# A state-space block feeding a gated feed-forward block: weights taken in every second column, output weights in rows of two, and an earlier order of loads

## The chip, the cores and the metric

The kernel runs on one core of one Trainium2 chip. The metric is device time in microseconds (us) of one execution; times given for a kernel are medians over its runs. A core has TensorE (PE in the profile; PEld is its loading of weights), VectorE (DVE), ScalarE (ACT), GpSimd (POOL) and SyncE (SP). SP, ACT and POOL also issue DMA transfers: SP and ACT on hardware queues, POOL on a software queue, which can convert the type on the way.

## The reference

First a chunked state-space scan over x (4 batches, 8 heads, 768 positions, 32 values per head), with a decay `a` per position and B and C of 16 values per position:

```python
L = np.exp(cum[:, :, :, None] - cum[:, :, None, :]) * causal
M = np.einsum('bhin,bhjn->bhij', Cc, Bc) * L
y_intra = np.einsum('bhij,bhjd->bhid', M, xc)
y_inter = np.einsum('bhin,bhnd->bhid', Cc, state) * decay_to_i[:, :, :, None]
y[:, :, sl] = y_intra + y_inter
```

The heads of a position are then laid side by side (3072 tokens of 256 values), and a gated feed-forward layer follows, with d_ff = 1536:

```python
gate = np.maximum(x @ w_gate, 0.0)
val = x @ w_val
out = gate * val @ w_out
```

Inputs and output are float32; the kernel computes in bf16 with float32 sums.

## The kernel before, in words

**Tiles.** The 3072 tokens are 12 *pairs* of 256 tokens (two chunks of 128), and 6 *blocks* of 512 tokens (two pairs). The scan is done by pairs, the feed-forward layer by blocks. d_ff is cut into 12 tiles `f` of 128 columns. `wg` and `wv` are the gate and value weights in SBUF, shaped [128, 2, 1536]: 128 partitions, the two halves `k` of d_model, and d_ff. `wo` is the output weights, [128, 12, 256].

**The scan of a pair p** is a row of small helpers: `scale_bc` scales B and C by the decay factors (DVE or POOL), `turn` transposes them on PE, `tevac` copies them out, `back` transposes B back, `G` multiplies C with B (8 matmuls), `gevac` masks the result (ACT copies quarters 0 and half of 1, which POOL masks at L174; DVE masks the others), `Dm` multiplies with x, `inter` adds the state, `yevac` writes the pair's columns of `yT`. `astep`, `states`, `sevac` and `spread` carry the state.

**The feed-forward layer of a block.** `gv(b, f)` makes gate and val of tile f for 512 tokens (L595, L598, two matmuls of 512 columns each, one for each half k); `gvh_mm(b, f, u)` does it for a half block of 256 tokens (L614, four matmuls), which the kernel uses where only one pair of a block is ready. ACT takes the relu, DVE multiplies into `h`. `fout(b, ts)` multiplies `h` with `wo` (L643), 12 tiles f for each 128 tokens.

**The order** is written out by hand: every engine's instructions run in the order in which the program emits them (`in_order`, L15). The stretch that the change touches is the opening (L677 to L809) and block 0 of the loop at L811. In the opening, pairs 0 and 1 are scanned, and the half blocks `gvh_mm(0, f, 0)` for f = 0 to 3 stand between their steps, so that PE has work: f = 0 ahead of `G(1)` (L765), f = 1 after it (L773). Block 0 then goes on with f = 0 to 3 of its other half, f = 4 to 11 with `gv`, and `fout`, between whose steps the scans of pairs 2 and 3 stand.

**The loads.** POOL issues the weights on the software queue, float32 to bf16: f 0-1 and 2-3 at L229, f 4-5 at L743, f 6-8 and 9-11 at L771, each as one transfer for gate and one for val, which covers both halves k; after that POOL scales B and C of pair 2 (L787) and issues the output weights in three transfers of four f (L788). Behind them it issues x of pair 2 (`cast_x`, L808), converted by the transfer itself. SP loads the other x, B and C as float32; `held` (L707) lets them wait for a small DVE memset. x is then cast by an engine (`x_cast`, `to_x`).

**Waits.** The framework sets the semaphores: for each instruction it compares what it reads and writes with what was emitted earlier, and lets it wait where they overlap. The transfers of the software queue use eight semaphores in turn.

Of the kernel before, what the change touches and what calls it, by code (L numbers as in the profile page):

```python
# [29 lines left out]
def kernel(  # L30
# [43 lines left out]
    def place(p):  # L74
        b, c0 = p // PPB, 2 * (p % PPB)
        return b, c0, slice(c0 * 128, (c0 + 2) * 128)
# [58 lines left out]
    def new_xb(p):  # L135
        xb = att.tile([128, 2 * NH * D], BF16, tag="xb", name="xb", bufs=6)
        st.setdefault(p, {})["x"] = [xb[:, i * NH * D:(i + 1) * NH * D] for i in range(2)]

    def cast_x(p):

        b, c0, sl = place(p)
        new_xb(p)
        for i in range(2):
            sl = slice((c0 + i) * 128, (c0 + i + 1) * 128)
            nc.gpsimd.dma_start(
                out=st[p]["x"][i].rearrange("s (h d) -> s h d", d=D),
                in_=x[b, :, sl, :].rearrange("h s d -> s h d"))

    ident = const.tile([128, 128], BF16)
    make_identity(nc, ident)  # L150

# [4 lines left out]
    def weights(f0, f1, which=(0, 1)):  # L156
        fs = slice(f0 * 128, f1 * 128)
        for k in which:
            w, src = ((wg, moe_w_gate), (wv, moe_w_val))[k]
            nc.gpsimd.dma_start(  # L160
                out=w[:, :, fs], in_=src[:, fs].rearrange("(k p) f -> p k f", k=2))

    def weights_out(f0, f1):
        nc.gpsimd.dma_start(
            out=wo[:, f0:f1, :],
            in_=moe_w_out[f0 * 128:f1 * 128, :].rearrange("(o i) m -> i o m", i=128))

    masks = const.tile([128, 2, 128], BF16)

# [286 lines left out]
    def sevac(p, i):  # L456
        c = 2 * p + i + 1
        if c == NC:
            return
        if c < 2 * NTILE:  # L460
            S[c] = n = att.tile([128, 64], BF16, tag="Sd", name="Sd")
            nc.scalar.copy(out=n, in_=A_ps[0][:, 0, 0:64])
        else:
            S[c] = spread_one(c, 0)
# [124 lines left out]

    def gv(b, f):  # L590
        tk = slice(b * 512, (b + 1) * 512)
        fs = slice(f * 128, (f + 1) * 128)
        g, v = bank("gate"), bank("val")
        for k in range(2):
            nc.tensor.matmul(out=g, lhsT=wg[:, k, fs], rhs=yT[:, k, tk],  # L595
                             start=(k == 0), stop=(k == 1))
        for k in range(2):
            nc.tensor.matmul(out=v, lhsT=wv[:, k, fs], rhs=yT[:, k, tk],  # L598
                             start=(k == 0), stop=(k == 1))
        r = ffn.tile([128, 512], BF16, tag="r", name="r", bufs=4)  # L600
        nc.scalar.activation(r, g, AF.Relu)  # L601
        nc.vector.tensor_tensor(out=fst[b][:, f], in0=r, in1=v, op=ALU.mult)  # L602

    def gvh_mm(b, f, u):
        if f == 0 and u == 0:
            fst[b] = ffn.tile([128, NF, 512], BF16, tag="h", name="h")
        tk = slice(b * 512 + u * 256, b * 512 + (u + 1) * 256)
        fs = slice(f * 128, (f + 1) * 128)
        gv_ = (mm.tile([128, 2, 256], FP32, tag="y", name="gv") if b + f == 0 else
               bank("gv", (128, 2, 256)))  # L610
        jk = [(j, k) for j in range(2) for k in range(2)]
        early = b + f + u == 0
        for j, k in sorted(jk, key=lambda v: v[1]) if early else jk:
            nc.tensor.matmul(out=gv_[:, j], lhsT=(wg, wv)[j][:, k, fs], rhs=yT[:, k, tk],  # L614
                             start=(k == 0 and not (early and j)), stop=(k == 1),
                             skip_group_check=True)
        fst[b, f, u] = gv_
# [81 lines left out]
    def x_cast(p, i, eng):  # L699
        copy(eng, st[p]["x"][i], st[p]["xr"][:, i].rearrange("s h d -> s (h d)"))  # L700
# [6 lines left out]
    def held(p, bc=True, with_x=True):  # L707

        if bc:
            new_bc(p)  # L710
            nc.vector.memset(st[p]["bcr"][0:1, 0, 1, 0, 0:1], 0.0)
            load_bc(p, 1, nc.sync)
            load_bc(p, 0, nc.sync)
        if with_x:
            new_x(p)
            if not bc:
                nc.vector.memset(st[p]["xr"][0:1, 0, 0, 0:1], 0.0)
            for i in range(2):
                load_x(p, i, nc.sync)
# [8 lines left out]

    gevac(0, between=lambda: backevac(0, nc.scalar), after={2: load_x1})
    held(2, with_x=False)  # L730
    d12 = mm.tile([128, 2, 2, 8], FP32, tag="tp", name="d12")
    dec_wide(d12, pick[:, 1:3, 0:8])
    nc.scalar.copy(out=wfac[:, 1:3, 1].rearrange("p w r h -> p r w h"), in_=d12)
# [7 lines left out]
    scale_bc(1, nc.vector, B_, ts=(0,))  # L741
    scale_bc(1, nc.gpsimd, B_, ts=(1,))
    weights(4, 6)  # L743
    new_xb(1)

    x_cast(1, 0, nc.gpsimd)
    Dm(0, "shared")
    inter(0, 1)
    astep(0, 1)
# [2 lines left out]
    yevac(0, nc.scalar, nc.vector)  # L752
    bevac(1, nc.scalar)
    cevac(1, nc.vector)
    sevac(0, 1)

    def turn(p):
        transp(p, 1)
        transp(p, 0)
# [8 lines left out]
    back(1)  # L768
    gevac(1, early=True, between=lambda: backevac(1, nc.scalar))
    x_cast(1, 1, nc.scalar)  # L770
    weights(6, 9)  # L771
    weights(9, NF)
    gvh_mm(0, 1, 0)  # L773
    gvh_relu(0, 1, 0)
    gvh_mm(0, 2, 0)
# [9 lines left out]
    nc.vector.reciprocal(wfac[:, 2:4, 0], wfac[:, 2:4, 1])  # L785
    new_bs(2)
    scale_bc(2, nc.gpsimd)  # L787
    weights_out(0, 4)  # L788
    weights_out(4, 8)
    weights_out(8, NF)  # L790
    Dm(1, "shared")
    inter(1, 0)
    inter(1, 1)
# [11 lines left out]
            out=fac[:, :, 2 * w:2 * w + 2, 1, :].rearrange("p b i h -> p i b h"),  # L805
            in_=dall[:, :, w])
    new_bs(3)
    cast_x(2)  # L808
    scale_bc(3, nc.gpsimd)  # L809

    for b in range(NBLK):  # L811
        P, Q, W = 2 * b + 2, 2 * b + 3, 2 * b + 1
        more = P < NPAIR
        for n in (P + 2, P + 3):
            if b and n < NPAIR:
                load(n, nc.sync)

        nh = (4, 6, 5)[min(b, 2)]
        for f in range(nh):
            if b == 0:  # L820
                continue
            turning = f == (3 if b == 1 else 2)
            gvh_mm(b, f, 0)
            gvh_relu(b, f, 0)
            gvh_mul(b, f, 0)
            if turning:
                inter(W, 0)
                inter(W, 1)
                Dm(W)
                if more:  # L830
                    states(P)
                yevac(W, nc.scalar)
                if more:
                    spread(P)
        for f in range(nh):
            gvh(b, f, 1)
        for f in range(nh, NF):
            gv(b, f)
            if b == 0:
                if f == 5:  # L840
                    over_sum(de)
                if f == 6:
                    turn(P)
                    tevac(P, nc.scalar, nc.vector)
                if f == 8:
                    sevac(1, 1)
                if f == 9:
                    held(Q, bc=False)
                    back(P)
                    backevac(P, nc.scalar)  # L850
            elif more:
                if f == max(5, nh):
                    turn(P)
                    tevac(P, nc.scalar, nc.vector)
                    scale(Q, nc.gpsimd)
                if f == 8:
                    turn(Q)
                    tevac(Q, nc.scalar, nc.vector)
                    if Q + 1 < NPAIR:
                        scale(Q + 1, nc.gpsimd)  # L860
        if more and b:
            inter(P, 0)
            inter(P, 1)
        if b == 0:

            for third in range(3):
                fs = range(4 * third, 4 * third + 4)
                fout(b, 0, fs)
                fout(b, 1, fs)
                if third == 0:  # L870
                    held(Q + 1)
                if third == 1:
                    G(P)
                    gevac(P)
                    to_x(Q, nc.gpsimd)
            turn(Q)
            tevac(Q, nc.scalar, nc.vector)
            foevac(b, 1)
            state(P, 0)
            state(P, 1)  # L880
            held(Q + 2)
            def recip(n):
                nc.vector.reciprocal(fac[:, n, :, 0], fac[:, n, :, 1])

            recip(1)
            fout(b, 2)
            back(Q)
            backevac(Q, nc.vector)
            recip(2)
            recip(3)  # L890
            inter(P, 0)
            inter(P, 1)
        else:
            fout(b, 0)
            foevac(b, 0)
            if more:
                G(P)
                gevac(P)
            fout(b, 1)
            foevac(b, 1)  # L900
            fout(b, 2)
            foevac(b, 2)
        if more:
            Dm(P)
            states(Q)
            yevac(P, nc.scalar)
            G(Q)
            spread(Q)
            gevac(Q)
            if b == 0:  # L910
                scale(Q + 1, nc.gpsimd)
            fout(b, 3)
            foevac(b, 3)
        else:
            fout_last(b)
# [32 lines left out]
```

## Time and profile before

| | |
|---|---|
| median of 3 runs | 127.87 us (126.57 to 130.34) |
| the profiled execution | 127.37 us, of which the span from its first to its last instruction is 125.6 us |
| PE, DVE, ACT, POOL busy | 119.2, 95.1, 79.5, 44.0 us |
| granted TensorE clock | 1.00 in every stretch |
| software queue (q0) | 6384 packets, 2.49 MB |
| hardware queue of SP (q1) | 64512 packets, 8.57 MB |

How to read the profile: times are from the span's start. The span is cut into 40 slices of 3.14 us, and a digit is the busy share of a slice in tenths. A line of the timeline has start, duration, engine, line of the kernel, operation, what it writes and reads, how many were merged (x8) and, in brackets, how long the engine stood idle before it and what released it. Matmuls overlap, so that the time from one start to the next says more than the duration of one. A line of the chain that ended last has start, duration and what the end of the program hung on in that time. "To landing" is the time from the issue of a transfer until its data are reported as there.

### The profile page before, as it was taken

How to read it: one execution, taken by the hardware profiler on the slowest of the kernel's cores; microseconds unless marked ns; L12 is line 12 of the kernel's file. 1: busy time of each engine (PE TensorE's matmuls, PEld its weight loads, DVE VectorE, ACT ScalarE, POOL GpSimd, SP SyncE). 2: the span in 40 equal slices, each digit the busy share in tenths (PEclk: the TensorE clock that was granted, in tenths of full speed). 3: DMA queues.
4: the chain of work that ended last, by engine and by line, in shares of the span. 5: the costliest groups of instructions: out<-in, count | busy, mean ns of one | idle time of the engine just before them, and what ended most of it. 6: DMA issues, size and time to landing. Idle time of an engine off the chain costs nothing.

```text
span 125.6 us, 3450 instructions
## 1 busy us (share of the span) xinstructions
PE 119.2 (95%) x1282; PEld 83.3 (66%) x1288; DVE 95.1 (76%) x236; ACT 79.5 (63%) x181; POOL 44.0 (35%) x83
## 2 busy tenths in 40 slices
PE   7899999978999999999999999999999999999990
PEld 2566844556886567885477885577874577864790
DVE  5888789939999955898865998865898856697510
ACT  4167876523888734888745787725887645886410
POOL 5869969404624153713102805021700033000000
PEclk9999999999999999999999999999999999999999
DMA  3999999998969998386952289912200002200022
GB/s 68 191 185 161 134 196 198 175 116 79 178 69 189 97 123 127 106 123 93 94 83 89 85 87 125 111 23 84 89 0 0 0 0 85 87 0 0 5 84 84
DMA packets 74464, 12.00 MB, mean 96 GB/s; under 512 B 67040, under 2 KB 74448, under 8 KB 74448
## 3 DMA queue, kind: packets, MB, share of 16 engines
q1 hardware_dynamic: 64512, 8.57, 43.2%
q0 software_dynamic: 6384, 2.49, 17.1%
q10 hardware_dynamic: 3552, 0.72, 2.8%
q8 instruction: 10, 0.16, 0.6%
q14 instruction: 6, 0.05, 0.1%
HBM read 11.12 MB, written 3.15 MB: 114 GB/s over the span
## 4 chain that ended last, share of the span: by engine, by line
PE 75%; DMA 14%; DVE 5%; POOL 2%; issue 1%; SPq 1%; ACT 0%; DVEq 0%; POOLq 0%
PE o L643 22%; PE gv L614 19%; PE val L598 12%; PE gate L595 11%; DMA wo<-in_moe_w_out_dram 6%; DMA bcr<-in_B_dram 5%; PE g L406 3%; DMA bcr<-in_C_dram 3%; PE y L569 3%; PE tp L342 2%; DVE gs L429 2%; PE y L558 2%; PE o L655 1%; DVE bs L310 1%; POOL bs L310 1%
## 5 line engine op out<-in xcount | busy, mean ns | idle before, releaser
L643 PE MATMUL o<-wo,h 128*128 128x256 bf16 x276 | 33.2, 273 | 1.1 <-DMA wo<-in_moe_w_out_dram 1.1
L602 DVE TENSOR_TENSOR h<-r,val 128x512 bf16<-128x512 bf16 x42 | 28.6, 685 | 5.2 <-ACT r L601 2.9
L643 PEld LDWEIGHTS <-h 128*128 128x128 bf16 x276 | 25.9, 98 | 6.6 <-issue 3.3
L601 ACT ACTIVATE r<-gate 128x512 bf16<-128x512 f32 x42 | 25.1, 597 | 7.8 <-PE gate L595 6.9
L624 DVE TENSOR_TENSOR h<-r,gv 128x256 bf16<-128x256 bf16 x60 | 24.5, 419 | 3.0 <-ACT r L621 2.3
L174 POOL TENSOR_SCALAR_AFFINE_SELECT gs<-gs 128x512 bf16<-128x512 bf16 (+1 forms) x24 | 12.1, 527 | 40.5 <-ACT gs L418 40.5
L598 PE MATMUL val<-yT,wv 128*128 128x512 bf16 x84 | 25.0, 379 | 0.5
L621 ACT ACTIVATE r<-gv 128x256 bf16<-128x256 f32 x60 | 22.9, 386 | 2.5 <-PE gv L614 0.3
L595 PE MATMUL gate<-yT,wg 128*128 128x512 bf16 x78 | 23.7, 379 | 0.0
L614 PE MATMUL gv<-yT,wg 128*128 128x256 bf16 x120 | 23.1, 273 | 0.0
L614 PE MATMUL gv<-yT,wv 128*128 128x256 bf16 x120 | 23.0, 273 | 0.0
L429 DVE TENSOR_TENSOR gs<-g,masks 128x512 bf16<-128x512 f32 x24 | 15.4, 683 | 6.8 <-PE g L406 6.8
L310 POOL TENSOR_TENSOR bs<-bcr,fac 128x256 bf16<-128x256 f32 x16 | 9.6, 620 | 16.1 <-DMA bcr<-in_B_dram 16.1
L598 PEld LDWEIGHTS <-wv 128*128 128x128 bf16 x84 | 8.1, 98 | 10.3 <-DMA wv<-in_moe_w_val_dram 0.6
L418 ACT CAST gs<-g 128x512 bf16<-128x512 f32 x12 | 7.1, 589 | 10.6 <-PE g L406 10.6
L614 PEld LDWEIGHTS <-wv 128*128 128x128 bf16 x120 | 11.7, 98 | 1.4
L614 PEld LDWEIGHTS <-wg 128*128 128x128 bf16 x120 | 11.2, 98 | 1.7 <-issue 0.2
L284 ACT CAST yT<-y 128x512 bf16<-128x512 f32 (+1 forms) x14 | 7.1, 527 | 7.7 <-PE y L569 4.5
L595 PEld LDWEIGHTS <-wg 128*128 128x128 bf16 x84 | 7.8, 98 | 6.3
L672 ACT COPY ob<-o 128x512 f32<-128x512 f32 x10 | 5.9, 586 | 4.2 <-PE o L643 4.2
L284 POOL CAST xb<-xr 128x512 bf16<-128x512 f32 (+1 forms) x11 | 6.3, 573 | 3.2 <-DMA xr<-in_x_dram 2.5
L368 DVE TENSOR_SCALAR CT<-tp,tmask 128x256 bf16<-128x256 bf16 x23 | 7.0, 343 | 0.1
(102 smaller groups left out, 111.5 us busy)
## 6 DMA issues: line engine op xcount, KB each, us to landing
xr<-in_x_dram SPq DMA_DIRECT2D x21, 128.0 KB, 3.3
out_dram<-ob SPq DMA_DIRECT2D x10, 256.0 KB, 2.2
bcr<-in_C_dram SPq DMA_DIRECT2D x16, 64.0 KB, 3.1
bcr<-in_B_dram SPq DMA_DIRECT2D x16, 64.0 KB, 3.0
wo<-in_moe_w_out_dram POOLq DMA_DIRECT2D x3, 256.0 KB, 7.0
bcr<-in_C_dram SPq DMA_DIRECT2D x3, 128.0 KB, 6.1
bcr<-in_B_dram SPq DMA_DIRECT2D x3, 128.0 KB, 6.3
wg<-in_moe_w_gate_dram POOLq DMA_DIRECT2D x3, 128.0 KB, 4.4
```

Of the source, the lines that this page charges most:

```text
L174: nc.gpsimd.affine_select(out=dst, in_=dst, pattern=pattern, compare_op=ALU.is_ge, fill=0.0, base=0, channel_multiplier=-1)
L284: (eng.copy if eng is nc.scalar else eng.tensor_copy)(out=out, in_=in_)
L310: eng.tensor_tensor(out=dst[:, :, t], in0=src[:, :, t], in1=f[:, :, 4 * t:4 * t + 4].to_broadcast([128, n, 4, N]), op=ALU.mult)
L429: nc.vector.tensor_tensor(out=d[:, q], in0=g[q], in1=m, op=ALU.mult)
L595: nc.tensor.matmul(out=g, lhsT=wg[:, k, fs], rhs=yT[:, k, tk], start=(k == 0), stop=(k == 1))
L598: nc.tensor.matmul(out=v, lhsT=wv[:, k, fs], rhs=yT[:, k, tk], start=(k == 0), stop=(k == 1))
L601: nc.scalar.activation(r, g, AF.Relu)
L602: nc.vector.tensor_tensor(out=fst[b][:, f], in0=r, in1=v, op=ALU.mult)
L614: nc.tensor.matmul(out=gv_[:, j], lhsT=(wg, wv)[j][:, k, fs], rhs=yT[:, k, tk], start=(k == 0 and not (early and j)), stop=(k == 1), skip_ ...
L621: nc.scalar.activation(r[:, 0:256], fst[b, f, u][:, 0], AF.Relu)
L624: nc.vector.tensor_tensor(out=fst[b][:, f, u * 256:(u + 1) * 256], in0=fst.pop((b, f, u, "r"))[:, 0:256], in1=fst.pop((b, f, u))[:, 1], op ...
L643: nc.tensor.matmul(out=o[:, ts % 2], lhsT=fst[b][:, f, ts * 128:(ts + 1) * 128], rhs=wo[:, f], start=(f == 0 and new), stop=(f == NF - 1), ...
```

## The change

- Tile f no longer takes 128 neighbouring columns of `wg` and `wv` but every second column of a group of 256: `tile_f(f)` is the slice that starts at 256 (f // 2) + f % 2 and has step 2. The rows of the output weights that belong to one partition of tiles 2g and 2g + 1 are then neighbours in memory, and `weights_out` moves two rows as one piece: 768 pieces of 2 KB at the source instead of 1536 of 1 KB.
- The weights come in groups of two f throughout (six groups, before five). Gate's f 6-7 is issued already with f 4-5, ahead of `G(1)`; val's f 6-7, then f 8-9, f 10-11 and the three transfers of the output weights follow at once after `gevac(1)`, ahead of POOL's scaling of pair 2.
- x of pair 2 is loaded by SP as float32, after B and C of pair 2, and cast by POOL (`to_x`); `cast_x` goes.
- The cast of the first half of x of pair 1 moves from POOL to DVE, behind `cevac(1)`.
- In block 0 the turn of pair 2 moves from f = 6 to f = 9, the evacuation of a state from f = 8 to f = 7, the transposing back of pair 2 from f = 9 to f = 11.

On each engine the changed kernel has the same work otherwise. Its line numbers are some five lower from `weights` on (L614 becomes L609, L643 becomes L638).

```diff
     def weights_out(f0, f1):
         nc.gpsimd.dma_start(
-            out=wo[:, f0:f1, :],
-            in_=moe_w_out[f0 * 128:f1 * 128, :].rearrange("(o i) m -> i o m", i=128))
+            out=wo[:, f0:f1].rearrange("p (g j) m -> p g (j m)", j=2),
+            in_=moe_w_out[f0 * 128:f1 * 128, :].rearrange("(g p j) m -> p g (j m)", p=128, j=2))
+
+    def tile_f(f):
+        return slice(f // 2 * 256 + f % 2, (f // 2 + 1) * 256, 2)
...
     def gv(b, f):
-        fs = slice(f * 128, (f + 1) * 128)
+        fs = tile_f(f)
...
     def gvh_mm(b, f, u):
-        fs = slice(f * 128, (f + 1) * 128)
+        fs = tile_f(f)
...
     held(2, with_x=False)
+    new_x(2)
+    for i in range(2):
+        load_x(2, i, nc.sync)
...
     weights(4, 6)
+    weights(6, 8, (0,))
     new_xb(1)
-    x_cast(1, 0, nc.gpsimd)
...
     cevac(1, nc.vector)
+    x_cast(1, 0, nc.vector)
     sevac(0, 1)
...
     x_cast(1, 1, nc.scalar)
-    weights(6, 9)
-    weights(9, NF)
+    weights(6, 8, (1,))
+    weights(8, 10)
+    weights(10, NF)
+    weights_out(0, 4)
+    weights_out(4, 8)
+    weights_out(8, NF)
...
     scale_bc(2, nc.gpsimd)
-    weights_out(0, 4)
-    weights_out(4, 8)
-    weights_out(8, NF)
+    to_x(2, nc.gpsimd)
...
     new_bs(3)
-    cast_x(2)
     scale_bc(3, nc.gpsimd)
...
             if b == 0:
-                if f == 6:
-                    turn(P)
-                    tevac(P, nc.scalar, nc.vector)
-                if f == 8:
+                if f == 7:
                     sevac(1, 1)
                 if f == 9:
                     held(Q, bc=False)
+                    turn(P)
+                    tevac(P, nc.scalar, nc.vector)
+                if f == 11:
                     back(P)
                     backevac(P, nc.scalar)
```

More of the change, by code (lines that the diff above doesn't have):

```diff
@@ L137, in new_xb @@
         st.setdefault(p, {})["x"] = [xb[:, i * NH * D:(i + 1) * NH * D] for i in range(2)]
[L139 to L147, printed above, removed]
     ident = const.tile([128, 128], BF16)
```

## The prediction

> **What bounds the kernel now.** I began with the busy shares and the 40 slices, to see which engine fills the span and where it does not.
>
> ```profile
> PE 119.2 (95%) x1282; PEld 83.3 (66%) x1288; DVE 95.1 (76%) x236; ACT 79.5 (63%) x181; POOL 44.0 (35%) x83
> PE   7899999978999999999999999999999999999990
> DMA  3999999998969998386952289912200002200022
> ```
>
> TensorE is busy 95% of the span; the DMA engines are full for the first 27 us (a slice is 3.14 us) and loose after that. So from about 27 us on nothing but TensorE's work counts, and whatever the change moves must pay in the first 27 us. Next, the list of waits of PE and the chain that ended last, in order of time:
>
> ```profile
> PE o L643 <- DMA wo<-in_moe_w_out_dram: 1.1, 1, 1.1
> ...
> PE y L558 <- DVE bcr L711: 0.4, 1, 0.4
> ```
>
> ```profile
> 18.03 0.76 POOL wo L164
> 18.79 7.04 DMA wo<-in_moe_w_out_dram
> 25.83 0.04 issue
> 25.87 1.03 PE o L643 x8
> ```
>
> The reader is to see that only one PE wait reaches 1 us: the second third of the output weights, issued by POOL at 18.79 and landed at 25.83. A smaller one stands in PE's timeline: a pair of 512-wide matmuls takes 0.43 us (17.08 to 17.51), yet 17.94 to 18.68 is 0.74, so 0.31 was lost, to val's weights.
>
> ```profile
> 10.32 0.27 PE L614 MATMUL gv<-yT,wg 128*128 128x256 bf16 x1
> 10.43 0.27 PE L614 MATMUL gv<-yT,wv 128*128 128x256 bf16 x1
> 10.54 0.27 PE L614 MATMUL gv<-yT,wg 128*128 128x256 bf16 x1
> ...
> 11.64 0.38 PE L614 MATMUL gv<-yT,wv 128*128 128x256 bf16 x2
> ...
> 17.08 0.59 PE L595 MATMUL gate<-yT,wg 128*128 128x512 bf16 x2
> 17.51 0.59 PE L598 MATMUL val<-yT,wv 128*128 128x512 bf16 x2
> 17.94 0.59 PE L595 MATMUL gate<-yT,wg 128*128 128x512 bf16 x2
> 18.68 0.60 PE L598 MATMUL val<-yT,wv 128*128 128x512 bf16 x2
> ```
>
> Last, POOL's timeline, since POOL issues the weights:
>
> ```profile
> 9.86 0.76 POOL L160 DMA_DIRECT2D wg<-in_moe_w_gate_dram  x1
> 10.62 0.72 POOL L160 DMA_DIRECT2D wv<-in_moe_w_val_dram  x1
> ...
> 12.03 1.04 POOL L174 TENSOR_SCALAR_AFFINE_SELECT gs<-gs 128x512 bf16<-128x512 bf16 x2
> 13.02 0.71 POOL L160 DMA_DIRECT2D wg<-in_moe_w_gate_dram  x1
> ```
>
> An issue takes 0.72 us of POOL, and those behind the masking of pair 1 wait for it. So the most that this change can save is the weight waits, 1.06 + 0.31 = 1.37 us.
>
> **The decisive part: the strided slice brings waits.** In the kernel before, f = 0 waits only for the weights of f = 0, 1, and f = 1 for nothing more. In the changed kernel as built, the weight loads of the first two tiles wait for this (software DMA semaphores go round in eights: 0, 1 are gate and val of f 0-1; 2, 3 of f 2-3; 4, 5 of f 4-5; 6, 7 of f 6-7; then 0, 1 again for f 8-9 and 2, 3 for f 10-11):
>
> ```
> f = 0, k = 1: Ldweights wg [waits DMASW6,DMASW4,DMASW2]
>               Ldweights wv [waits DMASW5,DMASW3]
> f = 1, k = 1: Ldweights wg [waits DMASW2 (second),DMASW0 (second)]
>               Ldweights wv [waits DMASW7,DMASW3 (second),DMASW1 (second)]
> POOL: DMACopy wv, f 6-7 [waits PE, f = 0's last matmul]
> ```
>
> No arithmetic needs them. They fit one reading: a slice with a step is compared by the outer bounds of both accesses. A transfer writes its columns in both halves k of a tile, so its bounds run from column c of half 0 to column c + 255 of half 1; the k = 1 slice of f = 0 or 1 lies inside these bounds for every c. So f = 0 waits for all weights issued ahead of it in the program (up to gate's f 6-7) and f = 1 for all of them.
>
> First wait. Gate's f 6-7 is issued at 11.34 (behind the two issues shown). Val's f 4-5 just ahead of it landed at 10.62 + 5.5 = 16.1, gate's f 4-5 at 9.86 + 5.1 = 15.0: 1.1 apart. So it lands at 16.1 + 1.1 = 17.2. Bounds: 16.1 (val's f 4-5 is waited for too) and 18.9 (11.34 + 7.6, the longest landing of a software transfer, the last third of the output weights). I take 17.2, by the nearest row. PE, at its third matmul (10.54 before), waits until then.
>
> Second wait. Behind f = 0 on PE are queued G(1) and back(1); ACT waits for G(1) to copy a quarter of it, POOL for ACT to mask it, and only then POOL issues the five other weight transfers. Before, 10.54 to 13.02 is 2.48 us for the same stretch; I add 0.4 for a slow PE (below), half of its some 0.8 us of matmuls again: 17.2 + 2.9 = 20.1 for val's f 6-7. The fifth starts 4 x 0.72 = 2.9 later, at 23.0, and lands in 4.3 us, as the 128 KB weight transfers at 3.84 to 6.16 did (median 4.3): 27.3. Bounds of that landing: 3.0 (B of pair 0, by ACT's queue) and 5.5 (val's f 4-5). f = 1's last val matmul, at 11.64 + 0.11 = 11.75 before, starts at 27.3: **+15.55**.
>
> Slow restart. PE stands still for 6.7 and then some 8 us. The trace of before has no such stop but has a start from rest: the first nine matmuls took 3.04 us, where six of 0.217 and three of 0.055 (four transposes in 0.22) are 1.47. So a start from rest loses 1.57 us. The granted clock reads 1.00 in that stretch too, so by that column alone the loss would be 0. Between 0 and 1.9 (half of the 3.7 us until 128-wide matmuls came 0.06 apart) I take the row of durations: **+1.6**.
>
> [...]
>
> What goes. Once f = 1 runs, all gate and val weights are there: **-0.31**. The output weights, issued right behind at 23.7, 24.4 and 25.2, land by 25.2 + 7.6 = 32.8 at the latest, and fout starts at about 23.78 + 15.5 = 39: **-1.06**. The 0.36 at 30.0 us (L558 behind DVE's spread of the state) stays: its chain starts with G(2) and is not touched.
>
> Edits that I cost at nothing, with their cover. The cast of x (pair 1, half 0), 0.28 us, moves from POOL to DVE; its x lands at 11.57 and the masking behind it on DVE would end some 0.45 late, under PE's stop; without the stop that 0.45 counts. POOL's room for it goes to one issue of 0.72. x of pair 2 leaves the software queue (two issues of 0.92 us, landings of 7.2) for two 128 KB loads on SP, ahead of pair 3's B and C, and a POOL cast of 0.61: read only after fout's second third, some 28 us later than it lands; its packets ahead of the weights are in the 1.1 above. The software queue now has six pairs of weights instead of five: one more issue pair, 1.4 us, counted in the 4 x 0.72. Output weights in 768 packets instead of 1536: their wait is gone either way. Turn, state and back of pair 2 move by one to three f within block 0: the same instructions; scale_bc(2) on POOL, now behind the output weights, ends near 27.1, its turn comes at about 37. Strided weight loads: 98 ns shown, under matmuls that come every 109 (256 wide) or 217 ns: nothing, unless they double (below).
>
> **Sum.** 125.6 + 15.55 + 1.6 - 0.31 - 1.06 = 141.4 us of span. The profiled execution took 127.37 for a span of 125.6, so 1.8 lies around it: 143.2, I say **143.1**. That execution is 0.5 under the median of 127.87; the three runs differ by 3.8, so I make nothing of that.
>
> **Rivals.**
> - *Each tile waits for its own weights after all* (the other side). Then the 1.37 goes and DVE's 0.45 comes: 127.4 - 1.37 + 0.45 = 126.5, within 2%. For it: the arithmetic needs no more. Against it: the waits stand in the built program, and gate's f 6-7 isn't even issued when PE asks (11.34 against 10.54). It decides only if these waits were met by 10.6 and 11.8. 5 in 100.
> - *No slow restart*: 143.1 - 2.0 = 141.1 (1.6, and the 0.4 ahead of POOL's issues). For it: the clock column. Against it: the opening's durations. 20 in 100.
> - *Crowding*: x of pair 2 enters while weights load, the first wait ends at 18.9: 143.1 + 1.7 = 144.8. For it: landings grew from 4.3 to 6 while both queues were full. Against it: at 13 to 16 us the two queues left gaps. 14 in 100.
> - *Strided loads become the bound.* The only strided weight loads now are 4-byte ones (L239: 64 columns, 209 ns; L247, contiguous: 128 columns in 191), 2.2 times as long a column. A load can't occupy more than the 56 ns at which L655's matmuls follow, each with its own load; 2.2 times that is 123, 14 over the pace of 109, 240 times: 143.1 + 3.4 = 146.5. Against it: 64-column loads are mostly fixed time. 6 in 100.
>
> **How the numbers follow.** The forecast holds 55 in 100, within some 1 us of 143.1; 20, 14, 6 and 5 go as above. Range: from 139.5 (no restart loss, and the landing of 4.3 shortened to 3.0) to 146.5 (strided loads, or crowding with a 5.5 landing: 146.0). What measurement can tell from no change is about 2%, 2.6 us: all but the first rival lie beyond it. Slower 0.95, same 0.04, faster 0.01 (for the first rival with DVE's 0.45 hidden and more).
>
> **What would show it.** In the changed profile: PE idle twice, from about 10.6 to 17 and 18.8 to 27 us, released by DMA wg and wv at the gvh line; POOL idle before its masking of pair 1 and the next weight issue near 20; 256-wide matmuls after each stop some 0.21 us apart instead of 0.11; no wait for wo; weight loads of wg and wv still near 98 ns; TensorE unchanged after block 0. I am wrong if PE passes f = 0 and 1 without a stop, if the stops end elsewhere by more than 1.5 us, or if the loads of wg and wv grow.

## The result, and the profile after

The changed kernel takes **143.2 us** (median of 4 runs, 142.78 to 144.41) against 127.27 for the kernel before (median of the 4 runs beside them, 126.57 to 130.34): 1.129 times as long, with a 95% interval of 1.117 to 1.141. Single executions of a kernel can come out some per cent longer with nothing changed (130.34 here); the ratios and intervals leave such runs out, the medians do not. The profiled execution took 142.99 us for a span of 141.2; the one before took 127.37 for 125.6.

The busy shares and the 40 slices of the changed kernel come first (a slice is now 3.53 us; in the row PEclk 9 stands for the full granted clock and 5 for half of it):

```profile
PE 122.9 (87%) x1282; PEld 85.2 (60%) x1288; DVE 94.3 (67%) x237; ACT 79.9 (57%) x181; POOL 43.7 (31%) x83
PE   7990400699999999999999999999999999999990
PEclk9997555558999999999999999999999999999999
DMA  3999829964038979992579424895220000200022
```

PE stands still in slices 4, 6 and 7, at about 11 to 16 and 18 to 25 us, and its clock is halved from slice 5 to slice 9 (in slices 4 and 10 for a part). Behind that the row of PE is as full as it was. The first row of the list of PE's waits names the transfer that ends the stops (us in total, times, longest):

```profile
PE gv L609 <- DMA wg<-in_moe_w_gate_dram: 13.5, 2, 7.8
```

Two waits at the matmuls of the half tiles (L609) take 13.5 us. The wait of 1.1 us for the output weights and the one of 0.4 for the spread state (L558), which stood in this list before, are both gone. PE's timeline shows where the two stand:

```profile
10.27 0.27 PE L609 MATMUL gv<-yT,wv 128*128 128x256 bf16 x1
16.18 0.37 PE L609 MATMUL gv<-yT,wg 128*128 128x256 bf16 x1 [5.64 <-DMA wg<-in_moe_w_gate_dram]
...
25.69 0.37 PE L609 MATMUL gv<-yT,wg 128*128 128x256 bf16 x1 [7.84 <-DMA wg<-in_moe_w_gate_dram]
26.44 0.37 PE L609 MATMUL gv<-yT,wv 128*128 128x256 bf16 x1 [0.17 <-issue]
...
30.43 0.63 PE L609 MATMUL gv<-yT,wv 128*128 128x256 bf16 x2
30.86 0.64 PE L609 MATMUL gv<-yT,wg 128*128 128x256 bf16 x2
```

The first stop is ahead of the third matmul of f = 0, the second inside f = 1, both at half k = 1 of the weights. The last two rows, each a pair of 256-wide matmuls, are 0.43 us apart, which is 0.215 for each matmul instead of 0.11: they run at half the clock (granted clock 0.50 from 13 to 32 us, last section), more than 4 us after PE has started again.

The chain from one stop to the other, from the list of the chain that ended by 27 us, in order of time (start, us, what):

```profile
11.17 4.87 DMA wg<-in_moe_w_gate_dram
...
16.18 0.58 PE gv L609 x2
16.76 0.58 PE g L401 x8
17.34 0.58 ACT gs L413
...
18.00 1.03 POOL gs L169 x2
...
21.11 4.44 DMA wg<-in_moe_w_gate_dram
```

One loop is to be seen here. PE waits for weights; ACT, which copies G(1), waits for PE; POOL, which masks it, waits for ACT; the next weights wait for POOL; and PE waits for those. Between the last two rows shown POOL issues one transfer in some 0.7 us. The last issue that counts is the fifth, val's, at 21.82 on POOL; it landed at 26.35, and the last val matmul of f = 1 started at 26.44.

To follow the lost time I set the start of the same matmul in both traces side by side:

| landmark on PE | before, us | after, us | shift | what the step added |
|---|---|---|---|---|
| third matmul of f = 0 | 10.54 | 16.18 | +5.64 | first stop |
| last val matmul of f = 1 | 11.75 | 26.44 | +14.69 | second stop, +9.05 |
| gate of f = 4 | 16.22 | 33.42 | +17.20 | slow clock, +2.51 |
| output product starts | 23.78 | 40.66 | +16.88 | val's wait gone, -0.32 |
| G(2) | 26.84 | 42.50 | +15.66 | wait for wo gone, -1.22 |
| half tiles of block 1 | 32.97 | 48.22 | +15.25 | wait at L558 gone, -0.41 |
| everything until 120 us | | | +15.25 | nothing |
| end of the span | 125.6 | 141.2 | +15.60 | last store, +0.35 |

All of the loss lies ahead of 33.4 us. From 48 us to the end every matmul that I compared comes 15.25 us later than before. Of the -1.22 the wait that the trace before records is 1.06, and of the -0.41 it is 0.36; the small rest of both is not traced.

### The profile page after: what moved, and what is told of

The parts are those of the page before. It is cut to its first block, busy times and chain, and to the rows that moved or that the text cites. A ratio compares the mean times of both kernels' runs of the same rounds, so it can differ in the third digit from the quotient of the medians.

```text
span 141.2 us, 3460 instructions
## 1 busy us (share of the span) xinstructions
PE 122.9 (87%) x1282; PEld 85.2 (60%) x1288; DVE 94.3 (67%) x237; ACT 79.9 (57%) x181; POOL 43.7 (31%) x83
## 4 chain that ended last, share of the span: by engine, by line
PE 81%; DMA 9%; POOL 4%; DVE 2%; issue 1%; ACT 1%; SPq 0%; DVEq 0%
PE o L638 22%; PE gv L609 21%; PE val L593 14%; PE gate L590 12%; DMA wg<-in_moe_w_gate_dram 7%; PE g L401 3%; PE y L564 3%; DMA a_sb<-in_a_dram 2%; PE tp L337 2%; POOL wv L150 1%; PE y L553 1%; POOL wg L150 1%; PE o L650 1%; POOL gs L169 1%; PE A_ps L503 1%
## 5 line engine op out<-in xcount | busy, mean ns | idle before, releaser
L609 PE MATMUL gv<-yT,wg 128*128 128x256 bf16 x120 | 24.6, 286 | 13.5 <-DMA wg<-in_moe_w_gate_dram 13.5
L638 PE MATMUL o<-wo,h 128*128 128x256 bf16 x276 | 33.0, 273 | 0.0
L638 PEld LDWEIGHTS <-h 128*128 128x128 bf16 x276 | 25.8, 98 | 5.2 <-issue 2.1
L609 PE MATMUL gv<-yT,wv 128*128 128x256 bf16 x120 | 24.6, 285 | 0.2 <-issue 0.2
L609 PEld LDWEIGHTS <-wg 128*128 128x128 bf16 x120 | 11.6, 101 | 16.0 <-issue 14.1
L593 PEld LDWEIGHTS <-wv 128*128 128x128 bf16 x84 | 8.2, 98 | 9.9
L305 POOL TENSOR_TENSOR bs<-bcr,fac 128x256 bf16<-128x256 f32 x16 | 9.6, 620 | 13.7 <-DMA bcr<-in_B_dram 10.5
L609 PEld LDWEIGHTS <-wv 128*128 128x128 bf16 x120 | 12.2, 101 | 2.4 <-issue 0.6
L279 DVE CAST yT<-y 128x256 bf16<-128x256 f32 x2 | 0.9, 440 | 10.5 <-PE y L544 10.5
```

The source lines that it names most:

```text
L279: (eng.copy if eng is nc.scalar else eng.tensor_copy)(out=out, in_=in_)
L305: eng.tensor_tensor(out=dst[:, :, t], in0=src[:, :, t], in1=f[:, :, 4 * t:4 * t + 4].to_broadcast([128, n, 4, N]), op=ALU.mult)
L638: nc.tensor.matmul(out=o[:, ts % 2], lhsT=fst[b][:, f, ts * 128:(ts + 1) * 128], rhs=wo[:, f], start=(f == 0 and new), stop=(f == NF - 1), ...
```

## The experiments

Three questions were open. Do the waits come from the *slice* (a strided slice compared by outer bounds, the theory of the prediction), from the new *order* of the issues, or from reading every second column as such? Is the part of the loss behind the stops one of the clock? And what are the other parts of the change worth without the stops? The letters in the expectations belong to the one in which they stand.

**Weights laid out by group (e1).** The changed kernel, with the two halves k of a group of 256 columns side by side, so that a transfer fills one unbroken stretch of a tile. The outer bounds of a strided slice then lie inside its own group:

```diff
-    wg = glob.tile([128, 2, DF], BF16)
+    wg = glob.tile([128, NF // 2, 2, 256], BF16)
...
-                out=w[:, :, fs], in_=src[:, fs].rearrange("(k p) f -> p k f", k=2))
+                out=w[:, g], in_=src[:, fs].rearrange("(k p) f -> p k f", k=2))
...
-        return slice(f // 2 * 256 + f % 2, (f // 2 + 1) * 256, 2)
+        return slice(f % 2, 256, 2)
```

> The changed kernel with one edit: the gate and value weights lie as [128, 6, 2, 256], group of two f before half k, so that the outer bounds of a transfer end at its own group; the slices keep their step of two, and order, loads and output weights are those of the change. Theory A (the cost is the waits that the strided slice brings, because accesses are compared by their outer bounds): neither stop of PE at f = 0 and f = 1, no wait for the output weights, the clock stays up; 127.4 - 1.4 + 0.45 = 126.5 us, between 125.5 and 127.5, ratio to the kernel before 0.985 to 1.0. Theory B (strided weight loads are slow themselves): 256-wide matmuls further apart than 0.109 us, above 129. Theory C (the new order of the loads crowds the queues): PE waits for weights between 11 and 24 us, above 128.5.

Measured: 126.78 us (12 runs, 126.25 to 127.22), 1.002 times the kernel before, interval 0.999 to 1.005. Both stops are gone, with every other part of the change kept. The slices of this kernel (3.12 us each):

```profile
PE   7999999979999999999999999999999999999990
DMA  2999999969999993389912599602200002200022
```

PE is full where the changed kernel stood still, and the granted clock falls only behind PE's last matmul (its mean is 0.996). So the slice, through its bounds in this layout, is what costs the 16.4 us between the two medians. Yet nothing is gained on the kernel before, though its weight waits are gone too: the 0.9 us that theory A took off (127.4 to 126.5) do not show. The first row of the waits of PE, and the transfers behind it (issues around 15 us: KB, us from issue to landing):

```profile
PE tp L338 <- POOL bs L306: 0.8, 1, 0.8
```

```profile
bcr<-in_C_dram SPq DMA_DIRECT2D x1, 128.0 KB, 10.8
bcr<-in_B_dram SPq DMA_DIRECT2D x1, 128.0 KB, 9.5
```

C and B of pair 3, issued at 14.45 and 16.35 behind x of pair 2, take 10.8 and 9.5 us to land (the median of such transfers in the trace before was 6.1 and 6.3); POOL stands 5.77 us for them until 25.99, and PE's turn of that pair waits 0.78. The DMA row is full to about 25 us, as before the change, and again later, where PE's list of waits names none of its transfers. In this one profiled execution 0.9 us of span is left over (124.7 against 125.6), which the medians don't confirm.

**Contiguous tiles (e2).** The changed kernel with its order of issues, but a tile f of 128 neighbouring columns and output weights of one row a packet:

```diff
-            out=wo[:, f0:f1].rearrange("p (g j) m -> p g (j m)", j=2),
-            in_=moe_w_out[f0 * 128:f1 * 128, :].rearrange("(g p j) m -> p g (j m)", p=128, j=2))
+            out=wo[:, f0:f1, :],
+            in_=moe_w_out[f0 * 128:f1 * 128, :].rearrange("(o i) m -> i o m", i=128))
...
-        return slice(f // 2 * 256 + f % 2, (f // 2 + 1) * 256, 2)
+        return slice(f * 128, (f + 1) * 128)
```

> The changed kernel with tiles of 128 neighbouring columns again and output weights in rows of one; the new order of loads and of block 0 is kept. Theory A: no stop of PE, within 0.7 us of e1_group_major, so near 126.5. Theory B (strided loads are slow): faster than e1_group_major by over 1 us. Theory C (the order costs): both of them above 128.5. If output weights in rows of two matter, PE waits for them here and not in e1_group_major.

Measured: 126.63 us (12 runs), 1.0014 times the kernel before, 0.998 to 1.005. It differs from e1 only in strided reads and in rows of two, and it is 0.15 us from e1. So the two together neither cost nor give anything that can be measured, and the order alone brings no stop. In its one profiled execution, the longest of the 12 (128.04 us), PE waits 0.3 us for the output weights, and in that of e1 it does not; in the times this does not show.

**The slice alone (e3).** The reverse: the kernel before, with its order of issues and transfers, given the strided slice and the rows of two.

```diff
...
-        fs = slice(f * 128, (f + 1) * 128)
+        fs = tile_f(f)
...
```

(These lines stand in `gv` and in `gvh_mm`; `tile_f` and `weights_out` are those of the change.)

> The kernel before with the strided slices and output weights in rows of two alone; the order of loads and of block 0 is that of before. Theory A: two stops. The first lasts until the weights of f 4-5 have landed (14.5 to 16.1 us); the second until the last of the four transfers issued after pair 1's masking has landed, at 25.2 (24.2 to 26.2), as f = 1 waits for all of them; with 2.5 for a slow restart 141.4 us, between 139.5 and 143. The theory that the new order of the loads makes the cost: near 127.5.

Measured: 141.22 us (4 runs), 1.117 times the kernel before, 1.109 to 1.125. PE's timeline has the stops:

```profile
14.69 0.37 PE L617 MATMUL gv<-yT,wg 128*128 128x256 bf16 x1 [3.98 <-DMA wg<-in_moe_w_gate_dram]
...
24.74 0.40 PE L617 MATMUL gv<-yT,wg 128*128 128x256 bf16 x1 [7.86 <-DMA wg<-in_moe_w_gate_dram]
```

The last val matmul of f = 1 follows at 25.71. With the old order the stops come at the same two places and end 1.49 and 0.73 us sooner (16.18 - 14.69, 26.44 - 25.71), because less stands ahead in the program: f = 0 waits here for the weights up to f 4-5, and f = 1 for four later transfers instead of five. The order moves the stops a little; the slice makes them. The second stop ended 0.5 us later than the 25.2 that was expected, and the restart behind it cost 1.32 us (last section) instead of 2.5, so that the time's closeness to the expected 141.4 is in part luck.

**A warm clock (e4).** The changed kernel with 27 matmuls of constants (128x512, results unused) queued ahead of f = 1, so that PE works through the second stop:

```diff
+        if b == 0 and u == 0 and f == 1:
+            for _ in range(27):
+                nc.tensor.matmul(
+                    out=gv_.rearrange("p j m -> p (j m)"),
+                    lhsT=nc.const_aps.tensor(1.0, [128, 128], BF16),
+                    rhs=nc.const_aps.tensor(1.0, [128, 512], BF16), start=True, stop=True,
+                    skip_group_check=True)
```

> The changed kernel with 27 matmuls of constants, 128x512, put on PE ahead of f = 1, into the same bank, before the tile's own matmuls start it anew; they compute nothing that is used. They run while PE would stand still in the second stop. Theory A1 (of the stops' cost 2.5 us come from TensorE's clock, which is down when PE resumes): the second stop ends at the same time, about 26.4, the matmuls after it come 0.11 us apart at once, and the time falls by 2.5, to 140.7. The theory that the 2.5 are other waits of the stretch after the second stop: 143.2, with the same gaps as without the matmuls. The 27 also show how long PE must work without a gap before the clock is back: if after 3.7 us, as at the start of the kernel before, they end near 25; if after 6.7, near 26.5.

Measured: 140.81 us (4 runs, 140.09 to 140.84), 1.1125 times the kernel before, 1.107 to 1.118, and 2.4 us less than the changed kernel, with 27 matmuls more. The timeline:

```profile
17.27 8.39 PE L610 MATMUL gv<-const-bfloat16-1.0 128*128 128x512 bf16 x27
...
26.44 0.27 PE L616 MATMUL gv<-yT,wv 128*128 128x256 bf16 x1 [0.45 <-issue]
26.55 0.38 PE L616 MATMUL gv<-yT,wg 128*128 128x256 bf16 x2
26.76 0.38 PE L616 MATMUL gv<-yT,wv 128*128 128x256 bf16 x2
```

The second stop ends at 26.44, to the hundredth as in the changed kernel; but from there pairs of matmuls are 0.21 us apart instead of 0.43. From this matmul to the gate of f = 4 it takes 4.31 us (26.44 to 30.75), against 6.98 in the changed kernel and 4.47 before. So the third step of the table is the clock's.

**x of pair 2 later (e5).** e1, with x of pair 2 loaded behind C and B of pair 3, to see whether the wait that e1 brought is one of order:

```diff
     held(2, with_x=False)
-    new_x(2)
-    for i in range(2):
-        load_x(2, i, nc.sync)
...
     held(3, with_x=False)
+    new_x(2)
+    for i in range(2):
+        load_x(2, i, nc.sync)
...
     scale_bc(3, nc.gpsimd)
+    to_x(2, nc.gpsimd)
```

(The cast of x, to_x(2), moves from behind scale_bc(2).)

> e1_group_major with x of pair 2 loaded by SP after B and C of pair 3 instead of ahead of them, and POOL's cast of it after the scaling of pair 3. In e1_group_major the weight waits are gone, yet PE waits 0.78 us for the turn of pair 3, whose B and C landed 9.5 and 10.8 us after their issue, behind x of pair 2 and beside the output weights. Theory A (that crowding took back what the weight waits gave): B and C of pair 3 land near 21 to 22, no wait at the turn of pair 3, time 0.5 to 0.8 below e1_group_major, 126.0 to 126.3. Theory B (B and C of pair 3 are late because of the output weights' earlier issue, whatever SP does with x): the wait stays over 0.5, time as e1_group_major.

Measured: 127.54 us (6 runs) beside 127.72 for the kernel before (11 runs), ratio 1.0051, 0.9985 to 1.0118: no gain. The wait at the turn is gone, and others stand in its place. Two of them in PE's timeline:

```profile
26.76 1.03 PE L639 MATMUL o<-wo,h 128*128 128x256 bf16 x8 [0.21 <-DMA wo<-in_moe_w_out_dram]
...
28.45 0.21 PE L444 MATMUL A_ps<-xb,bx 128*32 128x64 bf16 x4 [0.44 <-POOL xb L280]
```

C of pair 3 now lands at 20.3, but B still at 25.56 (10.2 us after its issue), and the two halves of x at 27.07 and 27.67 (11.1 us), late for their cast. Neither theory held whole: C landed early and the wait went, as A said, but B stayed late and no time was gained. The row of the DMA engines stands at 8 or 9 to about 34 us here, as in the kernel before; the order changed which transfer was late, and not the time.

**The old order with the repaired layout (e6).** The kernel before, with weights by group, strided slices, rows of two and weight transfers in twos of f, and nothing else of the change:

```diff
-    wg = glob.tile([128, 2, DF], BF16)
+    wg = glob.tile([128, NF // 2, 2, 256], BF16)
...
-        fs = slice(f * 128, (f + 1) * 128)
+        fs = tile_f(f)
...
-    weights(6, 9)
-    weights(9, NF)
+    weights(6, NF)
```

> The kernel before, its order of loads and of block 0, with the group-major weights in groups of two f, slices with a step of two and output weights in rows of two: what the tile form does without the new order and without the added waits. If strided loads and rows of two cost nothing and give nothing on the path: 126.75, ratio 0.995 to 1.005; the waits for val's weights and for the output weights remain, the latter shorter by up to 0.5 if rows of two travel faster, or longer by up to 0.7 if a sixth group of weights ahead of them counts more.

Measured: 126.74 us (6 runs), ratio 0.9998, 0.995 to 1.005. Both waits were expected to remain, and neither is in the trace: not the one for val's weights, and not the one for the output weights, though these are issued only at 18.45 to 19.91. Their three transfers took 5.7 us here (median), 7.0 before; whether that is the rows of two was not tested apart. Others take their place. The first of them is for a cast of x, for which ACT itself had waited 1.10 us until x landed:

```profile
13.83 0.35 PE L573 MATMUL y<-gs,xb 128*32 128x128 bf16 x12 [0.67 <-ACT xb L288]
...
29.62 0.28 PE L562 MATMUL y<-CT,Sm 128*128 128x128 bf16 x2 [0.33 <-DVE bcr L715]
```

**Transfers in halves (e8).** The changed kernel and its layout, but each weight transfer cut in two, one for each half k. A transfer's bounds then lie inside its own columns:

```diff
-            nc.gpsimd.dma_start(
-                out=w[:, :, fs], in_=src[:, fs].rearrange("(k p) f -> p k f", k=2))
+            for i in range(2):
+                nc.gpsimd.dma_start(out=w[:, i, fs], in_=src[i * 128:(i + 1) * 128, fs])
```

> The changed kernel with each transfer of gate and value weights cut in two, one for each half k, the layout kept. Theory A (outer bounds of a transfer that spans both halves): the bounds no longer reach into the first tiles' slices, PE has no stop of over 1 us at f = 0 and f = 1 and the clock stays up; but POOL issues 12 more transfers at 0.72 us, of which 4 come ahead of the cast of x of pair 0, so that the opening is late by some 2.7 us and the last weights by up to 6: 129 to 134. The theory that any strided slice waits for the whole tensor: both stops stay, over 143.

Measured: 129.07 us (2 runs, 128.88 and 129.26), ratio 1.0185, 1.0095 to 1.0274. There is no stop at f = 0 or 1 and the clock stays at 1.0. This tells the reading by bounds from a coarser one, in which a slice with a step waits for every write to its tile: the strided reads are still there, and the tile's layout is the changed kernel's. What remains is most likely the price of twice the issues on POOL: two halves take it some 1.1 us where one whole transfer took 0.72, and the chain that ended last runs through POOL's issues until 21.7 us. The opening is later by 0.7 us (the first matmul of f = 0 at 10.84 instead of 10.16) and not by the expected 2.7, and the time lies at the lower end of what was expected. Behind its start the longest waits of PE are now for engines, 0.9 and 0.6 us:

```profile
PE val L593 <- DVE h L597: 0.9, 1, 0.9
...
PE bt L382 <- DVE CT L363: 0.6, 1, 0.6
```

## Why the prediction was right, by its steps

The forecast was 143.1 us, the time 143.2. The mechanism stood as written; the closeness is in part luck, since two terms were off by almost the same amount in opposite directions.

| term | predicted, us | measured, us |
|---|---|---|
| stops, to the last val matmul of f = 1 | +15.55 | +14.69 |
| slow restart | +1.6 | +2.51 |
| val's wait | -0.31 | -0.32 |
| wait for the output weights | -1.06 | -1.22 |
| wait at L558 | 0 | -0.41 |
| end | 0 | +0.35 |
| sum, on the span of 125.6 | 141.4 | 141.2 |

- **The stops.** The first ends at 16.18, not at 17.2. The transfer that ends it, gate's f 6-7, landed 4.87 us after its issue at 11.17, where 17.2 - 11.34 = 5.9 was forecast from the landings in the old trace. There POOL went on to issue four transfers of weights at 13.02 to 15.15; in the changed kernel it issues none until 18.98. That this made the landing shorter is likely, but no run tests it. From the end of one wait to the end of the other it is 10.26 us (16.18 to 26.44) where 27.3 - 17.2 = 10.1 was forecast: POOL's issue came 2.80 after the first wait (forecast 2.9), the fifth issue 2.84 behind that (2.9), and it landed in 4.53 (4.3). POOL's timeline shows the two issues:

```profile
18.98 0.72 POOL L150 DMA_DIRECT2D wv<-in_moe_w_val_dram  x1
...
21.82 0.75 POOL L150 DMA_DIRECT2D wv<-in_moe_w_val_dram  x1
```

- **The slow restart** was sized from the opening, where 1.57 us are lost, and measured 2.51 here and 1.32 in e3 (last section). That a stop costs what the opening costs was an estimate: the trace before has no stop of this length. The rival without it, 141.1 us, is out: e4, which keeps the clock up through the second stop, takes 140.81, and the 2.4 us between it and the changed kernel are what the rival left out.

- **The wait at L558** was said to stay, since its chain is not touched. The chain's work isn't, but what runs beside it is. Before, then after, POOL's cast of x and DVE's reading of the state:

```profile
29.66 0.61 POOL L284 CAST xb<-xr 128x512 bf16<-128x512 f32 x1 [0.65 <-DVE CT L368]
29.70 0.84 DVE L485 TENSOR_TENSOR Sm<-carry,smask 128x256 bf16<-128x256 f32 x1
```

```profile
44.62 0.61 POOL L279 CAST xb<-xr 128x512 bf16<-128x512 f32 x1
45.37 0.42 DVE L480 TENSOR_TENSOR Sm<-carry,smask 128x256 bf16<-128x256 f32 x1
```

  Where the two ran side by side DVE's instruction took 0.84 us, and where POOL's was done 0.14 us before it took 0.42. The difference is just the wait that went. Of the sixteen times that this instruction runs in the two traces only one more took over 0.43 us: 1.18 at 22.39 before, beside POOL's scaling of B and C (22.02 to 23.27). That the two engines slow each other here is read from these rows, not tested by a run.

- **The tail**: from SP's last issue to the end it is 2.5 us instead of 2.16. The prediction left the end alone. The cause of this 0.35 stays open.

- **Strided loads as the bound** (146.5) is out on three counts: the weight loads of the strided tiles still take 98 ns, the shift stays at 15.25 us from 48 us to the end, and e1 and e2 agree. The 209 ns from which this rival started were read at 3.81 us, behind the opening's 128x512 matmuls, which took 626 ns against 379 later; at 7.53 us loads of 64 such columns from the same line take 138. Gate's weight loads in the full tiles of the changed kernel (busy us, mean ns of one, idle before); val's take the same 98:

```profile
L590 PEld LDWEIGHTS <-wg 128*128 128x128 bf16 x84 | 7.8, 98 | 6.5
```

- **Crowding** (144.8) was wrong for this kernel: x of pair 2, issued at 11.29 and 11.93, landed 4.97 us later each, and gate's weights landed sooner, not later. It came true where the stops were taken away: in e1, where the software queue runs on, C and B of pair 3 take 10.8 and 9.5 us.

- **Each tile waits for its own weights** (126.5) did not happen, but e1 is that kernel, and it takes 126.78. That this is near 126.5 is luck: the kernel before took 126.75 beside it, and the 0.9 us that the rival's sum took off did not come. DVE's 0.45 for the cast did not show (x was there at 10.78, DVE had waited 0.23), and the 0.8 us at the turn of pair 3 were not foreseen.

What the change was to save, 1.37 us at most, was there to be taken in three ways (e1, e2, e6), and none of them is faster than the kernel before by more than the interval. The waits for the weights were the last of a row: the DMA engines are full to 25 us and more (8 or 9 in their row from the second slice on) in the kernel before, in e1 and in e5, and in e1, e5 and e6 another transfer became the late one. The prediction's reading that they are loose from 27 us on is not what its row says, which has 8 or 9 in eight of the eleven slices from 28 to 63 us; it did no harm, since PE waits for none of those transfers.

## What to carry to other kernels

Before a slice with a step reads from a tile that is filled in parts, ask whether the outer bounds of each part's write overlap those of the slice; if the writes span an outer dimension of the tile, they can, as they did here for half k = 1, and the reader here waited for all of them (13.5 us in two waits). The cure cost nothing that could be measured here (e1): lay the tile out so that each transfer fills one stretch, and look at which semaphores the first reader waits for in the built program. And while the DMA engines were full, a transfer's place in the order only decided who waits (in e5 the 0.78 us at the turn went, and 0.21 and 0.44 us came elsewhere); count what becomes late next before moving one ahead.

## What the runs showed of the hardware that was not expected

**The clock fell 1.2 to 1.5 us after PE stopped and came back 3.4 to 6.1 us after PE's last gap.** Three windows of the changed kernel (from:to, length, busy us of PE, PEld, DVE, ACT, POOL, the granted clock, the DMA share, GB/s):

```profile
12.00:13.00 1.00, 0.00 (x0) 0.00 (x0) 0.00 (x0) 0.00 (x0) 0.00 (x0) 0.52 1.37 175
13.00:32.00 19.00, 7.81 (x76) 4.98 (x77) 3.67 (x10) 4.01 (x15) 8.49 (x13) 0.50 0.83 112
32.00:33.00 1.00, 1.00 (x9) 0.78 (x8) 0.42 (x1) 0.59 (x2) 0.00 (x0) 0.74 0.84 132
```

The clock record of the trace puts the edges at 12.04 and 32.52, 20.48 us apart. In e3 they are at 12.05 and 29.11 (17.06 apart), in e4 at 11.80 and 22.04 (10.24). The record of the changed kernel runs at the full clock for 6.83 us from its start (5.21 to 12.04) and for 109.23 us behind the stops (32.52 to 141.75). 20.48, 17.06, 10.24, 6.83 and 109.23 are 6, 5, 3, 2 and 32 times 3.413: a step of some 3.41 us between changes is an estimate from these five lengths, and what sets it is not shown. At the first stop the clock fell 1.2 to 1.5 us after PE's last matmul had ended (10.5 to 10.7 us). After the last matmul of the program it took 4.8 us in the trace before (122.73 to 127.51) and 3.8 in that of the changed kernel (137.98 to 141.75). What decides between 1.2 and 4.8 us was not tested.

In all three runs the clock came back while PE worked without a gap, but after different times: in e4 after 6.02 us (16.02 to 22.04); in e3 after 3.40 us (25.71 to 29.11; PE had started again at 24.74 and stood for 0.37 us ahead of 25.71); in the changed kernel after 6.08 us (26.44 to 32.52; PE had started again at 25.69 and stood for 0.17 us ahead of 26.44). If the estimate of 3.41 us holds, the clock of the changed kernel could have come back at 29.11, when PE had worked for 2.67 us since this gap; it came back at 32.52. So two stops that end 0.73 us apart lost 1.32 us (e3) and 2.51 us (after), and the prediction's 1.6 lies between the two. How much work brings the clock back stays open, since no run varied it by itself.

**The column of the granted clock starts late.** Its record begins at 4.63 us in the trace before and at 5.21 in the changed kernel; ahead of that the column reads 1.00, while the durations of the opening matmuls (626 ns against 379) say otherwise. The prediction weighed that column against the durations; there was nothing in the column to weigh. One of e3's four executions has a mean of 1.00 in this column and took 143.39 us all the same; no trace of it is kept, so what its clock did stays open.

**Some transfers of the hardware queue landed 9.5 to 11.1 us after their issue, beside the software queue.** In e1 the 128 KB loads that SP issued at 14.45 and 16.35 us take 10.8 and 9.5 us, and in e5 those at 15.38, 16.02 and some 16.6 us take 10.2, 11.1 and 11.1; in the changed kernel, where POOL had stopped issuing, two of the same size took 4.97. The full software queue is not the whole of it: in e5 the load of C at 14.97 took 5.3 us, and in the kernel before, where POOL issued weights at the same time, those at 10.40, 14.51 and 14.92 took 6.3 to 6.8. What sets the time was not tested.
